# q and k stacks by one transfer, row maxima by one transfer, in a gated attention and MLP kernel

## The chip, the cores and the metric

The kernel runs on one core of a Trainium2 chip. Times are device microseconds (us) of one execution. The engines are named as the profile names them: PE (matmul), PEld (its weight loads), DVE, ACT, POOL, and SP, which here only issues transfers. A transfer is issued by SP or ACT and is carried by the 16 DMA engines of the core.

## The reference

```python
def _A_ref(x, wqkv, wo):                      # x: 1 x 2048 x 512
    H = 32; Dh = 16; W = 256                  # 32 heads of 16 columns, a window of 256 keys
    q, k, v = split(x @ wqkv)                 # each 32 heads x 2048 x 16
    scores = einsum(q, k) * Dh ** -0.5        # masked to 0 <= i - j < 256
    p = softmax(scores)
    return concat(einsum(p, v)) @ wo

def _B_ref(x, w1, b1, w2, b2):                # LayerNorm, 512 -> 1792, GELU, 1792 -> 512
    return gelu(layernorm(x) @ w1 + b1) @ w2 + b2

g = sigmoid((x * gate_w).sum(-1, keepdims=True))
return g * _A_ref(x, ...) + (1 - g) * _B_ref(x, ...)
```

## The kernel before, in words

Every product is made of rounded high parts and remainders (high x high, high x low, low x high), so each operand exists twice. The program has three stages on PE.

**Stage 1, to about 143 us.** `qk_unit(g, t, c)` makes q (t = 0) or k (t = 1) of a group g of 8 heads for a chunk c of 512 tokens, `v_unit(b)` makes v for 128 tokens. Each is 12 matmuls of 512 columns: four with the high part of x and the high part of the weights, four with their low part, and four with the low part of x. `units` is the list of them in order, and `plan` says ahead of which unit a transfer or a fill is issued. For the last chunk of x (c = 3) three of the four low parts are made on POOL (`lo_part` in `load_x`), behind the fills that `masks` and `masks_first` put on POOL's queue; the first unit that reads them is the ninth of the list (`QK(0, 0, 3)`).

`qk_out` sends the high part (twice) and the low part of q or k to `qkd` in HBM. There, one head has 48 rows of 2048 tokens (16 high, 16 high or low, 16 low), and two gap rows of -1 behind them, so 50 rows a head. `gaps(g)` writes these gap rows once for each group, by two transfers, from a part of the stacks tile that `masks` has filled with -1. The calls of `gaps` stand ahead of units 8, 16, 20 and 24, those of `load_stacks` for the first heads ahead of units 11, 19, 29 and 44.

**Stage 2, attention with the first half of the MLP, to about 487 us.** The heads go in eight groups p of four: two pairs `pr`, and in a pair two heads `e`. The tile `qk` (128 partitions, four parts: q of pair 0 and 1, k of pair 0 and 1) holds the stacks: partitions 14 to 61 the 48 rows of the first head of a pair, 64 to 111 those of the second. `load_stacks(p, a, n)` brings n token columns of them, by two transfers of 98 partitions, one for k and one for q. `s_pair` makes the scores of 128 queries and takes their row maxima (DVE); `put_max` splits the maxima in high and low (POOL), turns them (DVE), sends them to HBM, and `rest` brings them back as two rows into the q stacks, by two transfers: one for the high rows (partitions 62 and 112), one for the low rows (63 and 113). `st_pair` makes the transposed scores with these two rows taken along (against the -1 of k), so that the maximum is subtracted in the product; `pv` multiplies by v. The string `ORDER` fixes the order on PE: S is an `s_pair`, T an `st_pair`, P a `pv`, f two matmuls of the MLP (`mlp1_unit`).

**Stage 3.** The second half of the MLP and the output projection.

PE's first scores, the `s_pair` calls for p = 0, stand in stage 1: those for the first block of queries ahead of unit 16, those that need the second and third chunk of stacks later (`ps_x` in the profile). SP issues transfers in the program's order, and eight semaphores are shared by the transfers of SP and ACT, so a transfer is issued after the one eight places ahead of it has landed.

Of the kernel before, what the change touches and what calls it, by code (L numbers as in the profile page):

```python
# [13 lines left out]
F32R = mybir.dt.float32r  # L14
# [5 lines left out]
S = 2048  # L20
D = 512
H = 32
DH = 16
F = 1792
DT = D // 128
KT = D // 64
FT = F // 128
C = 512
NCH = S // C
NB = S // 128  # L30
NG = 4
HG = H // NG
VW = 17
VR = 560
EPS = 1e-5
NEG = -3.0e38
U8 = mybir.dt.uint8
# [24 lines left out]
def gated_mix_kernel(ctx, tc: tile.TileContext, xt, x2, wq0, wqk, wv, wo, xa, gw, w1, w2, b1, b2, out):  # L62
    nc = tc.nc
    dve, act, pool, pe, sp = nc.vector, nc.scalar, nc.gpsimd, nc.tensor, nc.sync
    consts = ctx.enter_context(tc.tile_pool(name="consts", bufs=1))
    dram = ctx.enter_context(tc.tile_pool(name="dram", bufs=1, space=bass.MemoryType.DRAM))
# [3 lines left out]
    def nm(s):  # L70
        uid[0] += 1
        return f"{s}_{uid[0]}"
# [10 lines left out]
    def get(key, tag, bufs, shape, dt=F32):  # L83
        return left[key].tile(list(shape), dt, name=nm(tag), tag=tag, bufs=bufs)
# [3 lines left out]
    def t2(dt=F32, shape=(128, 512)):  # L88
        return get("work", "t", nt[0], shape, dt)
# [36 lines left out]
    def view(t, *ap, off=0):  # L126
        return bass.AP(tensor=t.tensor, offset=t.offset + off, ap=[list(x) for x in ap])

    def f32(t):
        return t.bitcast(F32)  # L130

    def lo_part(lo, src, hi, eng=dve):
        eng.tensor_tensor(out=lo, in0=src, in1=f32(hi), op=ALU.subtract)
# [25 lines left out]
    osc = dram.tile([8, 128, S], F32, name="osc")  # L159
    stat = dram.tile([2, 2, S // 2], F32, name="stat")  # L160
    hp = dram.tile([NCH, FT, 128, C], F32, name="hp")
    qkd = {(g, t): dram.tile([HG, 50, S], F32R, name=f"qk{g}_{t}") for g in range(NG) for t in range(2)}

    open_pool("w")
    open_pool("ring")
    qk = get("ring", "qk", 1, (128, 4, S), F32R)
    qs, ks = [qk[:, pr] for pr in range(2)], [qk[:, 2 + pr] for pr in range(2)]
    vs = get("ring", "v", 1, (128, NB, VR))
    tri = consts.tile([128, 2, 128], U8, name="tri")
# [33 lines left out]
    def masks():  # L203
        for t in qs:
            pool.memset(f32(t[:32]), 0.0)
        for k in ks:
            pool.memset(f32(k[96:128]), -1.0)
        one = small("scr", 2, (128, 256), BF16)
        pool.memset(one, 1.0)
        pool.affine_select(out=one[:, :128], in_=one[:, :128], pattern=[[-1, 128]], base=0, channel_multiplier=1,  # L210
                           compare_op=ALU.is_ge, fill=0.0)
        for e in range(2):
            pool.tensor_copy(tri[:, e], one[:, :128])
        pool.memset(wide, 0.0)
        pool.memset(rt, 0.0)
        pool.affine_select(out=wide[:, 128:], in_=wide[:, 128:], pattern=[[-1, 128]], base=0, channel_multiplier=1,
                           compare_op=ALU.is_ge, fill=NEG)

    def gaps(g):
        for t in range(2):  # L220
            sp.dma_start(f32(view(qkd[g, t], [50 * S, HG], [S, 2], [1, S], off=48 * S)), f32(ks[0][112:128]))

    wq, wvs, xh, xl = {}, [], [], []

# [77 lines left out]
    def qk_unit(g, t, c):  # L302
# [6 lines left out]
                n += 1  # L309
        qk_out(g, t, c, o)  # L310

    def qk_out(g, t, c, o):
        d = qkd[g, t]
        h, l = t2(F32R), t2(F32R)
        copy(h, o)
        lo_part(l, o, h)

        def put(eng, k, s):
            eng.dma_start(f32(view(d, [S, DH], [50 * S, HG], [1, C], off=k * DH * S + c * C)), f32(s))

        if g:
            put(act, 0, h)
        late = (2, 1, 1, 1)[c] if not g else 1
        after(late, lambda: [put(sp, k, h) for k in ((0, 1 + t) if not g else ())])
        after(late, lambda: put(sp, 2 - t, l))

    def double(g, c, t):
        fr, to = (f32(view(qkd[g, t], [S, DH], [50 * S, HG], [1, C], off=k * DH * S + c * C)) for k in (0, 1 + t))
        sp.dma_start(to, fr)

    def v_unit(b):
# [12 lines left out]
    def load_stacks(p, a, n):  # L344
        g, j = divmod(p, 2)
        held_cols[p] = a + n
        for t in (1, 0):
            src = view(qkd[g, t], [S, 98], [100 * S, 2], [1, n], off=4 * j * 50 * S + a)
            sp.dma_start(f32(qk[14:112, 2 * t:2 * t + 2, a:a + n]), f32(src))

    mxs, done = {}, set()

    def s_pair(p, qb, pr):
        if qb == 0 and pr == 0:
            mxs[p] = small("mx", 2, (128, 2, 2, NB))
        assert qb * 128 < held_cols[p]
        n = min(qb + 1, 3) * 128
        t0 = qb * 128 + 128 - n
        o = two()
        for e in range(2):  # L360
            r, k = ((0, 62), (64, 112))[e]
            pe.matmul(o[:, e, :n], qs[pr][r:k, qb * 128:qb * 128 + 128], ks[pr][r:k, t0:t0 + n],  # L362
                      start=True, stop=True)
        m = mxs[p][:, pr, :, qb]
        if qb < 2:
            for e in range(2):
                sc = small("scr", 2, (128, 256), BF16)
                dve.tensor_tensor_reduce(out=sc[:, :n], in0=o[:, e, :n], in1=wide[:, 256 - n:], scale=1.0, scalar=NEG,
                                         op0=ALU.add, op1=ALU.max, accum_out=m[:, e:e + 1])
        else:  # L370
            dve.copy_predicated(o[:, :, :128], tri, o[:, :, 256:384])  # L371
            dve.tensor_reduce(m, o[:, :, :256], mybir.AxisListType.X, ALU.max)  # L372
        if pr and qb % 4 == 3:
            put_max(p, qb - 3)

    def put_max(p, a):
        mx = mxs[p][:, :, :, a:a + 4]
        sm = {}
        md = dram.tile([2, 2, 2, 4, 128], F32R, name=nm("md"))

        def parts():
            m = sm["m"] = small("nm", 2, (128, 2, 2, 2, 4), F32R)
            pool.tensor_copy(m[:, 0], mx)
            lo_part(m[:, 1], mx, m[:, 0], pool)

        def turn():
            sm["s"] = small("ms", 2, (128, 32))
            dve.transpose(sm["s"], f32(sm["m"]).rearrange("p a b c d -> p (a b c d)"))

        def put(eng=None):  # L390
            (eng or (act if spot[0] > 99 else sp)).dma_start(f32(view(md, [32, 4], [128, 32], [1, 32])), sm["s"])

        def rest():
            done.add(("m", p, a // 4))
            for k in range(2):
                src = view(md, [512, 2], [1024, 2], [1, 512], off=2048 * k)
                sp.dma_start(f32(qk[62 + k:113 + k:50, :2, a * 128:a * 128 + 512]), f32(src))

        if spot[0] is None:
            parts()  # L400
            after(1, lambda: (turn(), put(sp)))
            after(3, rest)
        else:
            for n, fn in zip(CHAIN, (parts, turn, put, rest)):
                soon(n, fn)
# [75 lines left out]
    def stat_end(half):  # L481
# [4 lines left out]
        ri = r.bitcast(I32)  # L486
        dve.tensor_scalar(ve, m[:, :, 1], 1.0 / D, EPS, op0=ALU.mult, op1=ALU.add)
        dve.tensor_scalar(ri, ve.bitcast(I32), 1, None, op0=ALU.logical_shift_right)
# [299 lines left out]
    t = spare[0]  # L788
# [115 lines left out]
    for n in range(len(seq)):  # L904
        tick()
        for k in (n + 6,):
            c, f = item(k)
# [4 lines left out]
        c, f = item(n + 1)  # L912
# [6 lines left out]
        c, f = seq[n]  # L919
# [52 lines left out]
```

## Time and profile before

| | us |
|---|---|
| median of 3 runs (lowest, highest) | 689.19 (689.06, 690.45) |
| the profiled execution | 689.64 |
| its span, first to last instruction | 687.8 |
| PE busy | 681.1 |
| DVE, ACT, POOL busy | 476.4, 384.6, 265.9 |

1.8 us of the profiled execution lie outside its span. A span of a matmul in the profile has a modelled end, and matmuls overlap, so PE's busy time is no measure of its rate; its idle time is that in which no matmul was under way. Rows of the views read as: start, length, engine, line, operation, tiles out and in, shape; in brackets the idle time of the engine ahead of it, and who ended it.

### The profile page before, as it was taken

The numbers are of one execution on the slowest core, as the hardware profiler recorded it, in microseconds if no ns is written. First come the engines' busy times: TensorE is split into PE (matmuls) and PEld (weight loads), VectorE is DVE, ScalarE is ACT, GpSimd is POOL, SyncE is SP. The second block draws the span as 40 slices with busy tenths as digits, with TensorE's granted clock in tenths as the row PEclk, the third lists the DMA queues.
The fourth block names the chain that finished last, engine by engine and source line by source line (L and its number), as shares of the span: only waits on it lengthen the run. The fifth ranks groups of instructions, "written<-read, shape, count | busy, mean of one in ns | idle before, by whom it ended". The sixth has DMA issues, their size and how long they took to land.

```text
span 687.8 us, 15593 instructions
## 1 busy us (share of the span) xinstructions
PE 681.1 (99%) x5674; PEld 535.5 (78%) x5674; DVE 476.4 (69%) x970; ACT 384.6 (56%) x637; POOL 265.9 (39%) x622
## 2 busy tenths in 40 slices
PE   9999999999999999999999999999999999999997
PEld 6887777877768777877787777777787888888886
DVE  6737789968777787777686877855575545556454
ACT  6438453457677776877758777687633224123231
POOL 6800156426666664765656566568000000000000
PEclk9999999999999999999999999999999999999999
DMA  8998888786575767566676555527876450841801
GB/s 322 354 290 266 278 262 267 217 253 224 176 211 173 247 211 228 174 214 188 190 240 207 168 185 153 178 96 240 288 238 204 143 173 5 275 126 41 253 1 62
DMA packets 89620, 137.91 MB, mean 200 GB/s; under 512 B 13160, under 2 KB 36648, under 8 KB 89416
## 3 DMA queue, kind: packets, MB, share of 16 engines
q1 hardware_dynamic: 81384, 128.72, 59.1%
q10 hardware_dynamic: 8160, 8.19, 3.9%
q8 instruction: 45, 0.74, 0.4%
q14 instruction: 31, 0.25, 0.1%
HBM read 81.53 MB, written 54.30 MB: 197 GB/s over the span
## 4 chain that ended last, share of the span: by engine, by line
PE 96%; ACT 1%; DVE 1%; DMA 1%; issue 0%; POOL 0%; SPq 0%; DVEq 0%; ACTq 0%
PE ps_b L651 22%; PE ps_a L881 22%; PE ps_b L441 13%; PE ps_d L308 12%; PE ps_b L418 7%; PE ps_b L362 7%; PE ps_d L338 7%; PE ps_o L850 6%; PE ps_d L295 1%; PE ps_x L362 1%; DMA qk<-qk 1%; PE ps_x L279 1%; ACT x L420 0%; DVE us L895 0%; DVE us L889 0%; ACT pb L420 0%
## 5 line engine op out<-in xcount | busy, mean ns | idle before, releaser
L651 PE MATMUL ps_b<-x,w 64*128 64x512 f32 x1344 | 207.1, 393 | 0.0
L881 PE MATMUL ps_a<-x,t 128*128 128x512 f32 x648 | 150.2, 389 | 0.2 <-DVE t L711 0.2
L372 DVE TENSOR_REDUCE mx<-ps_b 128x2 f32<-128x512 f32 x208 | 144.1, 693 | 7.1
L881 PEld LDWEIGHTS ps_a<-x,t 128*128 128x128 f32 x648 | 121.5, 188 | 26.2 <-DVE t L711 0.6
L651 PEld LDWEIGHTS ps_b<-x,w 64*128 64x128 f32 x1344 | 127.4, 186 | 10.5 <-ACT x L136 0.3
L371 DVE COPY_PREDICATED ps_b<-tri,ps_b 128x256 f32<-128x256 uint8 x208 | 88.4, 425 | 52.7 <-PE ps_b L362 40.6
L422 POOL TENSOR_SCALAR_AFFINE_SELECT pa<-pa 128x256 f32<-128x256 f32 x192 | 74.2, 414 | 57.7 <-ACT pa L420 56.7
L420 ACT ACTIVATE pa<-ps_b 128x768 f32<-128x768 f32 x96 | 76.5, 813 | 24.7 <-PE ps_b L418 13.3
L418 PE MATMUL ps_b<-qk 50*128 50x384 f32 (+5 forms) x512 | 87.8, 339 | 0.1
L308 PE MATMUL ps_d<-x,w 128*128 128x512 f32 x360 | 84.7, 390 | 0.0
L362 PE MATMUL ps_b<-qk 62*128 62x384 f32 (+3 forms) x472 | 83.0, 345 | 1.0 <-DMA qk<-qk 0.8
L308 PEld LDWEIGHTS ps_d<-x,w 128*128 128x128 f32 x360 | 67.3, 188 | 14.5 <-issue 0.5
L420 ACT ACTIVATE pb<-ps_b 128x768 f32<-128x768 f32 (+2 forms) x96 | 66.2, 706 | 20.5 <-PE ps_b L418 9.7
L422 POOL TENSOR_SCALAR_AFFINE_SELECT pb<-pb 128x256 f32<-128x256 f32 x160 | 62.2, 415 | 37.4 <-ACT pb L420 36.9
L707 ACT ACTIVATE t<-t,b1s 128x512 f32<-128x512 f32 x56 | 38.6, 716 | 44.0 <-DMA t<-hp 43.6
L418 PEld LDWEIGHTS ps_b<-qk 50*128 50x128 f32 (+1 forms) x512 | 48.8, 184 | 16.0 <-issue 3.2
L422 POOL TENSOR_SCALAR_AFFINE_SELECT x<-x 128x256 f32<-128x256 f32 x128 | 49.3, 414 | 29.7 <-ACT x L420 29.3
L420 ACT ACTIVATE x<-ps_b 128x768 f32<-128x768 f32 x64 | 50.7, 813 | 14.0 <-PE ps_b L418 9.7
L362 PEld LDWEIGHTS ps_b<-qk 62*128 62x128 f32 (+1 forms) x472 | 45.1, 184 | 17.2 <-issue 3.9
L338 PE MATMUL ps_d<-wv,x 128*128 128x512 f32 x192 | 46.7, 394 | 0.0
L850 PE MATMUL ps_o<-w,t 128*128 128x512 f32 x192 | 46.1, 389 | 0.0
L441 PE MATMUL ps_b<-pa,v 128*32 128x128 f32 (+2 forms) x704 | 42.9, 345 | 0.3 <-ACT x L420 0.2
(96 smaller groups left out, 757.1 us busy)
## 6 DMA issues: line engine op xcount, KB each, us to landing
qk<-qk SPq DMA_DIRECT2D x112, 196.0 KB
t<-hp SPq DMA_DIRECT2D x56, 256.0 KB
hp<-t SPq DMA_DIRECT2D x54, 256.0 KB
qk<-t SPq DMA_DIRECT2D x48, 256.0 KB
osc<-x SPq DMA_DIRECT2D x31, 256.0 KB
t<-in_w SPq DMA_DIRECT2D x28, 256.0 KB
w<-w SPq DMA_DIRECT2D x28, 256.0 KB
qk<-t ACTq DMA_DIRECT2D x24, 256.0 KB
```

The lines of the kernel that those rows point to most:

```text
L308: pe.matmul(o, a[:, dt * 128:(dt + 1) * 128], b[:, dt * C:(dt + 1) * C], start=n == 0, stop=n == 11)
L338: pe.matmul(o, x[:, a:a + 128], wvs[dt][:, k], start=n == 0, stop=n == 11)
L362: pe.matmul(o[:, e, :n], qs[pr][r:k, qb * 128:qb * 128 + 128], ks[pr][r:k, t0:t0 + n], start=True, stop=True)
L371: dve.copy_predicated(o[:, :, :128], tri, o[:, :, 256:384])
L372: dve.tensor_reduce(m, o[:, :, :256], mybir.AxisListType.X, ALU.max)
L418: pe.matmul(o[:, e, :w], ks[pr][r:k, kb * 128:kb * 128 + 128], qs[pr][r:k, kb * 128:kb * 128 + w], start=True, stop=True)
L420: act.activation(pt[:, :, :w], o[:, :, :w], AF.Exp, scale=0.25)
L422: pool.affine_select(out=pt[:, :, a:a + 128], in_=pt[:, :, a:a + 128], pattern=[[0, 2], [sgn, 128]], base=b, channel_multiplier=-sgn, comp ...
L441: pe.matmul(a[32 * h:32 * h + 32, at:at + w], vs[:, kb, v:v + 32], pts[p, kb][:, h, fr:fr + w], start=n == 0, stop=n == len(parts) - 1, sk ...
L651: pe.matmul(o[:, e], w[kt // 4][r:r + 64, k, m:m + 128], y[r:r + 64, a:a + C], start=n == 0, stop=n == 23)
L850: pe.matmul(a, x[:, g], wos[g][:, k], start=n == 0, stop=n == 11)
L881: pe.matmul(accs[c][b], x[:, b * 128:(b + 1) * 128], w, start=f == 0 and n == 0, stop=f == FT - 1 and n == 2)
```

## The change

The HBM arrays of q and k of a group become one array, with 52 rows a head (four gap rows). Its heads are ordered anew, by the order of the columns of the weights, so that the four parts q0, q1, k0, k1 of four heads lie at one stride. `load_stacks` brings all four parts by one transfer of 100 partitions: 14 to 61 the first head, 62 to 65 the gap rows, 66 to 113 the second head. The maxima use the gap rows 62 to 65 (high and low of the first head, high and low of the second), so `rest` is one transfer of four partitions. Only the four heads of a group that lie first in a stack have their gap rows written: `gaps` takes rows of 0 for q from partitions 0 to 3 of the stacks tile, and rows of -1 for k from partitions 124 to 127, all four parts of each. So `masks` fills partitions 96 to 127 of all four parts of the tile with -1, by one instruction, where it filled those of the two k parts by two.

```diff
+HR = 52
-    qkd = {(g, t): dram.tile([HG, 50, S], F32R, name=f"qk{g}_{t}") for g in range(NG) for t in range(2)}
+    qkd = [dram.tile([2, HG, HR, S], F32R, name=f"qk{g}") for g in range(NG)]
     def masks():
         for t in qs:
             pool.memset(f32(t[:32]), 0.0)
-        for k in ks:
-            pool.memset(f32(k[96:128]), -1.0)
+        pool.memset(f32(qk[96:128]), -1.0)
     def gaps(g):
         for t in range(2):
-            sp.dma_start(f32(view(qkd[g, t], [50 * S, HG], [S, 2], [1, S], off=48 * S)), f32(ks[0][112:128]))
+            dst = view(qkd[g], [S, 4], [2 * HR * S, 4], [1, S], off=(t * HG * HR + 48) * S)
+            sp.dma_start(f32(dst), f32(qk[124 * t:124 * t + 4]))
+    def rows(g, t, c, k):
+        return view(qkd[g], [S, DH], [HR * S, HG], [1, C], off=(t * HG * HR + k * DH) * S + c * C)
     def qk_out(g, t, c, o):
         def put(eng, k, s):
-            eng.dma_start(f32(view(d, [S, DH], [50 * S, HG], [1, C], off=k * DH * S + c * C)), f32(s))
+            eng.dma_start(f32(rows(g, t, c, k)), f32(s))
     def load_stacks(p, a, n):
         g, j = divmod(p, 2)
         held_cols[p] = a + n
-        for t in (1, 0):
-            src = view(qkd[g, t], [S, 98], [100 * S, 2], [1, n], off=4 * j * 50 * S + a)
-            sp.dma_start(f32(qk[14:112, 2 * t:2 * t + 2, a:a + n]), f32(src))
+        src = view(qkd[g], [S, 100], [4 * HR * S, 4], [1, n], off=2 * j * HR * S + a)
+        sp.dma_start(f32(qk[14:114, :, a:a + n]), f32(src))
     def s_pair(p, qb, pr):
-            r, k = ((0, 62), (64, 112))[e]
+            r, k = ((0, 62), (64, 114))[e]
     def put_max(p, a):
-        md = dram.tile([2, 2, 2, 4, 128], F32R, name=nm("md"))
+        md = dram.tile([4, 2, 4, 128], F32R, name=nm("md"))
         def parts():
             m = sm["m"] = small("nm", 2, (128, 2, 2, 2, 4), F32R)
-            pool.tensor_copy(m[:, 0], mx)
-            lo_part(m[:, 1], mx, m[:, 0], pool)
+            mt = mx.rearrange("p r e b -> p e r b")
+            pool.tensor_copy(m[:, :, 0], mt)
+            lo_part(m[:, :, 1], mt, m[:, :, 0], pool)
         def rest():
-            for k in range(2):
-                src = view(md, [512, 2], [1024, 2], [1, 512], off=2048 * k)
-                sp.dma_start(f32(qk[62 + k:113 + k:50, :2, a * 128:a * 128 + 512]), f32(src))
+            sp.dma_start(f32(qk[62:66, :2, a * 128:a * 128 + 512]), f32(view(md, [1024, 4], [512, 2], [1, 512])))
# in kernel(), the columns of the weights
-    wqk = A_wqkv[:, :2 * D].reshape(DT, 128, 2, NG, HG, DH).transpose(3, 2, 1, 0, 5, 4)
+    wqk = A_wqkv[:, :2 * D].reshape(DT, 128, 2, NG, 2, 2, 2, DH).transpose(3, 2, 1, 0, 7, 5, 4, 6)
```

On POOL the fills of `masks`, and what stands behind them up to the low parts of x (x is the pair of tiles with the high and the low part, v the tile that holds the raw x at that time, qk the stacks), stood in this order before:

```order
L205 MEMSET qk_79 32x2048 x2
L207 MEMSET qk_79 32x2048 x2
L209 MEMSET scr_273 128x256
L210 ISA
L210 AFFINE_SELECT scr_273<-scr_273 128x128
L213 CAST tri<-scr_273 128x128 x2
L214 MEMSET wide 128x256
L215 MEMSET rt 128x32
L216 AFFINE_SELECT wide<-wide 128x128
L583 MEMSET v_80 128x2240
L133 TENSOR_TENSOR x_33_157<-v_80,x_32_156 128x512 x3
```

and now:

```order
L206 MEMSET qk_75 32x2048 x2
L207 MEMSET qk_75 32x8192
L209 MEMSET scr_268 128x256
L210 ISA
L210 AFFINE_SELECT scr_268<-scr_268 128x128
L213 CAST tri<-scr_268 128x128 x2
L214 MEMSET wide 128x256
L215 MEMSET rt 128x32
L216 AFFINE_SELECT wide<-wide 128x128
L584 MEMSET v_76 128x2240
L134 TENSOR_TENSOR x_33_153<-v_76,x_32_152 128x512 x3
```

Nothing changed places; the second fill is one of 8192 columns in place of two of 2048.

On SP, from the second group's gap rows (qk_0_67 and qk_1_68 are its q and k in HBM, qk_79 the stacks tile) to the second chunk of stacks, it was:

```order
L221 DMA qk_0_67<-qk_79 8x2x2048
L221 DMA qk_1_68<-qk_79 8x2x2048
L468 DMA t_588<-in_xa 128x512
L319 DMA qk_1_70<-t_619 16x8x512
L468 DMA t_627<-in_xa 128x512
L468 DMA t_646<-in_xa 128x512
L319 DMA qk_0_71<-t_676 16x8x512
L349 DMA qk_79<-qk_1_66 98x2x512
L349 DMA qk_79<-qk_0_65 98x2x512
```

and it is now:

```order
L222 DMA qk_66<-qk_75 4x4x2048 x2
L469 DMA t_582<-in_xa 128x512
L322 DMA qk_67<-t_613 16x8x512
L469 DMA t_621<-in_xa 128x512
L469 DMA t_640<-in_xa 128x512
L322 DMA qk_68<-t_670 16x8x512
L351 DMA qk_75<-qk_65 100x4x512
```

The gap transfers stay two, with another shape; the two transfers of the stacks became one at the place of the first.

More of the change, by code (lines that the diff above doesn't have):

```diff
@@ L310, in qk_unit @@
         qk_out(g, t, c, o)
+    def rows(g, t, c, k):
+        return view(qkd[g], [S, DH], [HR * S, HG], [1, C], off=(t * HG * HR + k * DH) * S + c * C)
     def qk_out(g, t, c, o):
-        d = qkd[g, t]
         h, l = t2(F32R), t2(F32R)
@@ L327, in double @@
     def double(g, c, t):
-        fr, to = (f32(view(qkd[g, t], [S, DH], [50 * S, HG], [1, C], off=k * DH * S + c * C)) for k in (0, 1 + t))
+        fr, to = (f32(rows(g, t, c, k)) for k in (0, 1 + t))
         sp.dma_start(to, fr)
```

## The prediction

> **What bounds the kernel now.** I read the page's busy times and the chain that ended last first, then who PE waited for.
>
> ```profile
> PE 681.1 (99%) x5674; PEld 535.5 (78%) x5674; DVE 476.4 (69%) x970; ACT 384.6 (56%) x637; POOL 265.9 (39%) x622
> PE 96%; ACT 1%; DVE 1%; DMA 1%; issue 0%; POOL 0%; SPq 0%; DVEq 0%; ACTq 0%
> PE ps_x L279 <- DVE t L275: 1.3, 1, 1.3
> PE ps_b L362 <- DMA qk<-qk: 0.8, 1, 0.8
> PE ps_b L441 <- ACT x L420: 0.2, 1, 0.2
> PE ps_a L881 <- DVE t L711: 0.2, 1, 0.2
> ```
>
> PE is 96% of the chain, and of its waits (the last four rows are the whole list) one is for a transfer that the change touches: 0.8 us for a stack. No row says that PE waits for maxima. So the merging can give PE back 0.8 us at most, however much it saves on SP's queue. A loss has no such bound: what PE reads can come later. I therefore look for what comes later, and the place is stage 1, where the DMA engines are busiest (columns: window, its length, busy time and count of PE, PEld, DVE, ACT, POOL, granted clock, DMA share, GB/s):
>
> ```profile
> 10.00:20.00 10.00, 10.00 (x46) 8.29 (x45) 10.00 (x14) 5.91 (x11) 9.38 (x6) 1.00 1.05 401
> 30.00:34.00 4.00, 4.00 (x20) 3.30 (x19) 1.38 (x2) 1.51 (x3) 3.15 (x2) 1.00 0.84 258
> 34.00:40.00 6.00, 6.00 (x28) 4.99 (x27) 1.81 (x3) 1.52 (x3) 0.00 (x0) 1.00 0.87 232
> 40.00:50.00 10.00, 10.00 (x47) 8.01 (x45) 3.02 (x6) 2.62 (x6) 0.00 (x0) 1.00 0.99 310
> 50.00:60.00 10.00, 10.00 (x48) 7.86 (x48) 7.30 (x25) 8.59 (x22) 0.00 (x0) 1.00 0.93 287
> 60.00:72.00 12.00, 12.00 (x56) 9.08 (x55) 9.40 (x28) 7.37 (x18) 2.55 (x11) 1.00 0.91 287
> 72.00:100.00 28.00, 28.00 (x128) 21.48 (x127) 20.71 (x43) 17.15 (x43) 7.85 (x18) 1.00 0.84 251
> 100.00:108.00 8.00, 8.00 (x37) 6.36 (x37) 7.32 (x14) 2.79 (x6) 6.12 (x9) 1.00 0.87 293
> ```
>
> PE has no idle time from 10 to 108 us, and a DMA share of 0.84 to 0.99 leaves little room to catch up.
>
> **Part 1: the fill of -1 on POOL.** Two fills of 2048 columns become one of 8192.
>
> ```profile
> L583 POOL MEMSET v<- 128x2240 f32 x4 | 7.8, 1978 | 6.2 <-DMA v<-in_xt 6.2
> L207 POOL MEMSET qk<- 32x2048 f32 x2 | 3.6, 1808 | 0.1
> 16.04 3.56 POOL L207 MEMSET qk<- 32x2048 f32 x2
> 21.98 1.98 POOL L583 MEMSET v<- 128x2240 f32 x1
> 25.07 4.25 POOL L133 TENSOR_TENSOR x<-v,x 128x512 fp32r<-128x512 f32 x3 [1.11 <-ACT x L136]
> 28.08 3.11 PE L308 MATMUL ps_d<-x,w 128*128 128x512 f32 x13
> ```
>
> 2048 columns take 1.808 us, 2240 take 1.978: time goes with the columns, so 8192 take about 7.15 us, 3.6 more than the 3.56 of the pair. What stands behind it on POOL runs without idle time to 23.96; the low parts of x waited 1.1 us for ACT, so they move by 3.6 - 1.1 = 2.5 us and end at 29.3 + 2.5 = 31.8. The unit at 28.08 (a matmul each 0.227 us: 2.72 for 12) reads the low parts in its last four, the third of them in its 11th, at 28.08 + 10 x 0.227 = 30.35. PE waits 1.4 us, or 1.0 if the three take 1.3 us each. I take **1.3 us**, near certain as a mechanism. Nothing covers it: PE's queue is in order.
>
> **Part 2: the gap rows.** Eight transfers of 128 KB, two a group, read 4 partitions (32 KB of each) where they read 16. The destination's outer count goes from 8 to 4. The page of the profile has no time to landing for them, so I bound one.
>
> ```profile
> 28.77 1.50 SPq L221 DMA_DIRECT2D qk<-qk  x2
> 55.38 1.39 SPq L221 DMA_DIRECT2D qk<-qk  x2
> 65.32 2.25 SPq L221 DMA_DIRECT2D qk<-qk  x2
> 78.14 1.37 SPq L221 DMA_DIRECT2D qk<-qk  x2
> DMA packets 55, 0.14 MB, mean 283 GB/s; under 512 B 10, under 2 KB 10, under 8 KB 47
> q1 hardware_dynamic: 21, 0.08, 97.4%
> ```
>
> The last two rows are for 80.9 to 81.4 us, behind the fourth group's issue. Eight packets (55 - 47) are of 8 KB, and only these transfers have such; SP's queue, q1, spent 97.4% x 16 x 0.5 = 7.8 us on its packets, so at most 0.97 us on one of 8 KB. At the rate of 10 to 20 us (401 / 16 / 1.05 = 24 GB/s an engine) it would be 0.34. So the packets wait for something that is not the engine, and what eight engines share there is a block of 16 partitions. Estimates: before, 8 engines with two packets each, 0.7 to 1.9 us a transfer. After, four engines with four packets each: 1.4 us if the engine is the limit, and 4 x 1.94 = 7.8 if a partition gives no more than now (a quarter of the partitions, the same bytes). The 0.97 is nearer to a shared source than the 0.34, but it was taken beside other traffic; I take the middle of each, 1.3 before and 4.6 after: 2 x 3.3 = **6.6 us more a group** on the engines that carry them (ends: 2 x 0.7 = 1.4, 2 x 5.9 = 11.8).
>
> [...]
>
> **Part 3: what the stacks in stage 1 then cost PE.** A stack cannot be issued before its gap rows have landed, and stands behind them in the same queue.
>
> ```profile
> 40.74 0.88 SPq L349 DMA_DIRECT2D qk<-qk  x2
> SPq L468 <- DMA qk<-qk: 1.1, 1, 1.1
> 47.17 0.33 SPq L468 DMA_DIRECT2D t<-in_xa  x1
> 49.93 0.44 PE L362 MATMUL ps_x<-qk 62*128 62x128 f32 x4
> 62.69 1.05 SPq L349 DMA_DIRECT2D qk<-qk  x2
> 74.72 0.61 PE L362 MATMUL ps_x<-qk 62*128 62x384 f32 x4
> 94.94 1.06 SPq L349 DMA_DIRECT2D qk<-qk  x2
> 107.79 0.61 PE L362 MATMUL ps_x<-qk 62*128 62x384 f32 x4
> ```
>
> The wait row is for 45 to 48 us: SP waited to 47.17 for the first half of the first stack. The second half, issued 0.4 us behind, landed between 47.6 and 49.9: slack 1.1 (0 to 2.3), some 8 us from issue. By the same 8 us the second stack has 12.0 - 8 = 4 us of slack, the third 12.9 - 8 = 5. A merged stack of about 800 KB saves an issue (0.4 us sooner); if its bytes lie on fewer engines it is later, up to the 1.6 us that lie between two halves of equal size at most. I take 0.6 later. What is idle on the DMA engines takes up lateness: up to 60 us by the share, since 0.99 at 310 GB/s shows that the engines are occupied well under their best rate; behind that by the mean of what share and rate (of 401) leave.
>
> - To 49.9: 6.6 + 0.6 - 1.5 (16% of 30 to 34, 13% of 34 to 40, 1% of ten) = 5.7 late; less 1.1 of slack, PE is **4.6** behind. The 1.3 of part 1 lies inside: PE arrives later at the same wait.
> - To 74.7: 5.7 + 6.6 + 0.6 - 0.7 - 2.3 (19% of 12) = 9.9; less 4 = **5.9** behind.
> - To 107.8, two groups: 9.9 + 13.2 + 0.6 - 7.4 (26.5% of 28) - 1.6 = 14.7; less 5 = **9.7** behind.
>
> Beyond that there are no more gap rows, and the fourth stack (needed at about 150) has time. With the share alone throughout, 14.4; with the rate alone, nothing is left but part 1's 1.3.
>
> **Part 4: stage 2.**
>
> ```profile
> 222.32 2.14 SPq L349 DMA_DIRECT2D qk<-qk  x4
> 222.80 5.36 DMA qk<-qk
> 228.29 0.44 PE L362 MATMUL ps_b<-qk 62*128 62x384 f32 x2 [0.79 <-DMA qk<-qk]
> L349 SPq DMA_DIRECT2D qk<-qk x120: 308/411/2010, 40.7 to 447.5; - x120
> L397 SPq DMA_DIRECT2D qk<-md x64: 596/636/972, 81.3 to 465.8; - x64
> ```
>
> 60 issues of 0.41 and 32 of 0.64 us go: 45 us of SP's queue. They buy PE the 0.79 at best, at 228, where the second half (issued at 222.80, chain row) came last. One transfer is issued at 222.32, 0.5 sooner, but lands as a whole: -0.8 to +0.8, I take **+0.4**. The maxima come back 0.64 sooner; no PE wait hangs on them: 0, and if they came late, `st_pair` would be next to wait. Two more rows in the product, strided POOL copies of 16 columns and the new order of heads: 0, since matmul time goes with columns, and POOL has 61% idle to hide the copies; without that cover, 32 x under 0.1 us.
>
> **Sum.** 9.7 + 0.4 = 10.1 on the profiled execution's 689.64 (span 687.8 and 1.8 around it), which is 0.45 above the median 689.19: against the median, **699.3 us**.
>
> **Rivals.**
>
> - *The gap transfers are no slower than their engines (1.4 us a group more), or hide in idle DMA time.* For it: by the rate, 287 of 401 GB/s, engines are idle 28% at 50 to 72. Against: 0.97 against 0.34 us a packet. PE is left with part 1 and part 4: 1.3 + 0.4, to 4: 691 to 693.
> - *The other side, not slower: POOL's longer fill does no harm and only the wait at 228 goes.* It needs the third low part by 30.35, so the fill would have to cost under 3.6 - 1.4 = 2.2 us more. Then -0.8: 688.4, inside 0.2%. [...] No row of a PE wait leaves more than the 0.8 to gain by it.
> - *The gap transfers at their upper end, 11.8 a group.* Then 5.2 more for each of four groups: about 30 us, 719. For it: the 0.97 row. Against: that row has ACT's traffic beside it.
>
> **How the numbers follow.** A run can tell about 0.2% (1.4 us) from no change. The forecast, 5 to 16 us lost, has 0.60; the first rival 0.18; the upper end, above 16, 0.12; no loss 0.10. Part 1 alone (690.5) is at the bound of what is measured. Range: from 691, part 1 and little else, to 711, which leaves most of the upper end out. Slower 0.87 (all but the last case and a part of the first rival), same 0.10, faster 0.03.
>
> **What would show it.** Part 1: a PE wait of 1.0 to 1.5 us for POOL near 30 us, behind a fill of 7.1 us. Part 2: a low GB/s behind each pair of gap transfers. Part 3: PE waits for `qk<-qk` at the first three stacks, `ps_x` rows at about 54.5, 80.6 and 117.5 in place of 49.9, 74.7 and 107.8, and the attention stage no longer than before. I am wrong if those rows move by the same small amount: then the gap transfers are not slow, or other idle time takes them up.

## The result, and the profile after

| | before | after |
|---|---|---|
| median, us (lowest to highest, runs) | 689.19 (688.97 to 690.45, 5) | 718.14 (715.11 to 720.10, 5) |
| the profiled execution, its span | 689.64, 687.8 | 715.11, 713.1 |

The changed kernel takes 1.0408 times as long, with a 95% interval of 1.0381 to 1.0435: 29 us slower. I had forecast 699.3 us, between 691 and 711. The direction was right, the size was wrong by a factor of nearly three; 719, the figure of the third rival, is where the time came out. The profiled execution is the fastest of the five, so the 25.3 us that are read from its trace below are the smaller end of the loss.

PE's share of the chain and the list of who PE waited for answer to the first rows of the prediction (the last row of the list, of 0.2 us, left out):

```profile
PE 76%; DMA 13%; DVE 6%; ACT 2%; SPq 1%; issue 1%; ACTq 0%; POOL 0%; DVEq 0%
PE ps_x L364 <- DMA qk<-qk: 10.3, 2, 7.1
PE ps_d L309 <- ACT v L137: 3.1, 1, 3.1
PE ps_x L364 <- DVE mx L374: 2.2, 2, 1.6
PE ps_b L364 <- DMA qk<-qk: 1.3, 2, 0.8
PE ps_x L280 <- DVE t L276: 1.3, 1, 1.3
PE ps_d L341 <- DVE wv L236: 0.8, 1, 0.8
PE ps_b L442 <- POOL pb L423: 0.4, 1, 0.4
PE ps_b L364 <- DVE mx L370: 0.3, 1, 0.3
```

PE went from 96% of the chain to 76%, and where one row spoke of the stacks with 0.8 us, two now hold 11.6. The other new rows, for ACT and for DVE, name engines that the change hardly touches. The windows of stage 1 (columns as in the prediction) show where it happens:

```profile
30.00:34.00 4.00, 4.00 (x19) 3.33 (x18) 3.20 (x2) 1.50 (x4) 4.00 (x3) 1.00 0.97 303
34.00:40.00 6.00, 6.00 (x28) 4.96 (x27) 1.98 (x3) 2.31 (x4) 2.47 (x2) 1.00 0.50 116
40.00:50.00 10.00, 10.00 (x46) 8.29 (x45) 1.12 (x2) 1.20 (x2) 0.00 (x0) 1.00 0.69 206
50.00:60.00 10.00, 2.91 (x15) 2.10 (x13) 3.02 (x6) 2.02 (x5) 0.00 (x0) 0.84 0.99 273
60.00:72.00 12.00, 12.00 (x49) 9.45 (x50) 8.51 (x31) 9.90 (x25) 0.00 (x0) 0.85 0.74 230
72.00:100.00 28.00, 24.76 (x104) 18.48 (x103) 14.52 (x36) 12.02 (x30) 3.27 (x15) 0.94 0.69 200
100.00:108.00 8.00, 8.00 (x37) 6.20 (x37) 3.36 (x7) 2.02 (x5) 0.00 (x0) 1.00 0.51 111
108.00:143.00 35.00, 29.68 (x125) 22.56 (x124) 27.68 (x44) 15.33 (x33) 18.94 (x25) 0.95 0.81 249
```

Three things are to be seen. Behind the first pair of gap transfers, 34 to 40, the DMA engines' rate is 116 GB/s where it was 232; at 100 to 108, behind the last pair, it is 111 where it was 293. PE stands still for 7.1 of the ten microseconds from 50 to 60. And the granted clock, 1.00 before, is 0.84 to 0.94 from 50 to 100 and 0.95 from 108 to 143: at 60 to 72 PE is busy throughout and yet does 49 matmuls where it did 56, at 12 / 56 = 0.214 us each 1.5 us lost. By the clock itself PE loses 0.15 x 12 + 0.06 x 28 + 0.05 x 35 = 5.2 us in the three windows from 60 to 72, 72 to 100 and 108 to 143.

The first S of each of the four stacks, and what stood ahead of it in the timeline of PE and of SP's queue:

```profile
23.29 7.73 PE L341 MATMUL ps_d<-wv,x 128*128 128x512 f32 x24 [0.76 <-DVE wv L236]
32.50 1.04 SPq L222 DMA_DIRECT2D qk<-qk  x2
33.60 4.33 SPq L229 DMA_DIRECT2D t<-in_wqk  x1
38.02 5.21 SPq L322 DMA_DIRECT2D qk<-t  x3
48.76 0.31 SPq L351 DMA_DIRECT2D qk<-qk  x1
59.87 0.47 PE L364 MATMUL ps_x<-qk 62*128 62x128 f32 x2 [7.09 <-DMA qk<-qk]
89.44 0.62 PE L364 MATMUL ps_x<-qk 62*128 62x384 f32 x4 [3.22 <-DMA qk<-qk]
113.24 5.99 PE L309 MATMUL ps_d<-x,w 128*128 128x512 f32 x18 [3.14 <-ACT v L137]
131.99 0.62 PE L364 MATMUL ps_x<-qk 62*128 62x384 f32 x4
174.90 0.44 PE L364 MATMUL ps_b<-qk 62*128 62x384 f32 x2 [0.84 <-DMA qk<-qk]
```

The first S come at 59.87, 89.44, 131.99 and 174.90, where they were at 49.93, 74.72, 107.79 and, in the row below, 149.63: 9.9, 14.7, 24.2 and 25.3 us behind. The span is 713.1 - 687.8 = 25.3 longer, so all of the loss is made in stage 1, and the stages behind it took as long as before.

```profile
149.63 0.34 PE L362 MATMUL ps_b<-qk 48*128 48x384 f32 x2
```

In SP's queue the two issues of the gap transfers (L222) are followed by one issue of 4.33 us and three of 5.21; before, what followed took 1.38 and 2.51. What SP issues next stands still too: the stack is issued at 48.76 where it was at 40.74, and from 50 to 60, while PE waits for it, the DMA engines are full again (0.99).

### The profile page after: what moved, and what is told of

It is laid out like the page before. It is cut to its first block, busy times and chain, and to the rows that moved or that the text cites. A ratio compares the mean times of both kernels' runs of the same rounds, so it can differ in the third digit from the quotient of the medians.

```text
span 713.1 us, 15508 instructions
## 1 busy us (share of the span) xinstructions
PE 688.7 (97%) x5674; PEld 537.8 (75%) x5674; DVE 479.6 (67%) x970; ACT 384.3 (54%) x637; POOL 270.5 (38%) x621
## 4 chain that ended last, share of the span: by engine, by line
PE 76%; DMA 13%; DVE 6%; ACT 2%; SPq 1%; issue 1%; ACTq 0%; POOL 0%; DVEq 0%
PE ps_a L882 21%; PE ps_b L652 20%; PE ps_b L442 12%; PE ps_b L419 7%; PE ps_b L364 6%; PE ps_o L851 6%; DMA t<-in_xa 4%; DMA qk<-qk 3%; DMA t<-in_x 2%; PE ps_d L309 2%; PE ps_d L341 2%; DMA t<-in_wqk 2%; DVE x L134 1%; DVE t L533 1%; DVE wv L236 1%
## 5 line engine op out<-in xcount | busy, mean ns | idle before, releaser
L882 PEld LDWEIGHTS ps_a<-x,t 128*128 128x128 f32 x648 | 121.6, 188 | 25.3
L423 POOL TENSOR_SCALAR_AFFINE_SELECT pa<-pa 128x256 f32<-128x256 f32 x192 | 74.2, 414 | 56.3 <-ACT pa L421 55.3
L309 PE MATMUL ps_d<-x,w 128*128 128x512 f32 x360 | 89.6, 406 | 3.1 <-ACT v L137 3.1
L309 PEld LDWEIGHTS ps_d<-x,w 128*128 128x128 f32 x360 | 70.5, 197 | 19.5 <-ACT v L137 3.6
L421 ACT ACTIVATE x<-ps_b 128x768 f32<-128x768 f32 x64 | 50.7, 813 | 15.0 <-PE ps_b L419 10.9
L341 PE MATMUL ps_d<-wv,x 128*128 128x512 f32 x192 | 48.5, 399 | 1.1 <-DVE wv L236 0.8
L341 PEld LDWEIGHTS ps_d<-wv,x 128*128 128x128 f32 x192 | 35.4, 188 | 11.9 <-DVE wv L236 2.0
```

Of the source, the lines that this page charges most:

```text
L309: pe.matmul(o, a[:, dt * 128:(dt + 1) * 128], b[:, dt * C:(dt + 1) * C], start=n == 0, stop=n == 11)
L341: pe.matmul(o, x[:, a:a + 128], wvs[dt][:, k], start=n == 0, stop=n == 11)
L421: act.activation(pt[:, :, :w], o[:, :, :w], AF.Exp, scale=0.25)
L423: pool.affine_select(out=pt[:, :, a:a + 128], in_=pt[:, :, a:a + 128], pattern=[[0, 2], [sgn, 128]], base=b, channel_multiplier=-sgn, comp ...
L882: pe.matmul(accs[c][b], x[:, b * 128:(b + 1) * 128], w, start=f == 0 and n == 0, stop=f == FT - 1 and n == 2)
```

## The experiments

The theory after this trace was: the gap transfers, read from four neighbouring partitions, are slow at their source; while a pair of them runs, nearly all other transfers stand still, and the idle time that they leave cannot be used. The rivals were that the count of engines (four for the gap rows, ten for the merged stacks) is what is slow, that SP's queue is, or that the merged transfers have a price of their own. A second theory was for the fill on POOL. All are compared with the kernel before, run on the same chip.

Two readings below go beyond the views: the trace also keeps when the semaphore of a transfer goes up. Apart from a step as the issue ends, where there is one, the semaphore of a gap transfer goes up in eight steps in the kernel before, in four in after, and in sixteen where the transfer reads 64 partitions; that of a stack goes up in fourteen steps for each half before and in ten in after. For the gap transfers before and after these are the counts of engines that the prediction reckons with, so I take the steps as the engines that carry a transfer, which is an estimate of mine, and the last step as its landing (the first stack's in after comes at 59.82, PE's first S at 59.87). From the first issue to the landing of both, the first pair of gap transfers takes 5.5 us before (28.77 to 34.26) and 12.0 in after (32.50 to 44.50).

| kernel | median, us | ratio to before (95%) |
|---|---|---|
| before + gap rows from four neighbouring partitions | 721.34 | 1.0463 (1.0421 to 1.0505) |
| before + gap rows, destination written as four pieces | 690.14 | 1.0007 (0.9988 to 1.0026) |
| before + one long fill | 693.23 | 1.0039 (1.0021 to 1.0057) |
| after, gap rows from 64 partitions | 694.32 | 1.0073 (1.0053 to 1.0094) |
| after, gap rows from every fourth partition | 698.71 | 1.0117 (1.0072 to 1.0162) |
| after, gap rows in pieces of 2 KB, from four neighbouring partitions | 720.07 | 1.0426 (1.0373 to 1.0478) |
| after, gap rows issued by ACT | 720.27 | 1.0429 (1.0381 to 1.0478) |
| after, the fill in four | 720.54 | 1.0438 (1.0399 to 1.0477) |
| after, further matmuls in PE's waits | 717.83 | 1.0393 (1.0345 to 1.0441) |
| after, gap rows from 64 partitions, no long fill | 691.20 | 1.0013 (0.9996 to 1.0030) |
| the same, stacks of q and k apart | 690.38 | 0.9999 (0.9985 to 1.0013) |
| the same as the last but one, maxima by two | 693.91 | 1.0049 (1.0025 to 1.0072) |

**Is it the gap rows alone?** Into the kernel before, only the gap transfers were put that the change has, which read four neighbouring partitions on four engines:

```diff
-            sp.dma_start(f32(view(qkd[g, t], [50 * S, HG], [S, 2], [1, S], off=48 * S)), f32(ks[0][112:128]))
+            dst = view(qkd[g, t], [100 * S, 4], [50 * S, 2], [S, 2], [1, S], off=48 * S)
+            src = view(qk, [list(qk.ap)[0][0], 4], [0, 2], [1, 2 * S], off=124 * list(qk.ap)[0][0] + 2 * S)
+            sp.dma_start(f32(dst), f32(src))
```

> The kernel before, with one thing changed: the two gap transfers of each group read four partitions (each one's 4 x 2048 values of -1 twice over the same two stacks) and start on four engines, as in the changed kernel; stacks, maxima and the fill stay as before. Theory (the slow gap transfers carry nearly all of the loss: 25.3 us less 2.8 us of the fill): 706 to 714 us, the gap transfers land some 10 us after issue (5.3 before), and the first S of stage 1 comes 6 to 10 us later than at 49.93. Rival (the gap transfers cost the 7 us that I forecast, and the rest is the merged loads with their ten engines): 695 to 699 us.

Measured: 721.34 us, with stacks, maxima and the fill as before. The gap rows by themselves cost as much as the whole change. That is above the 714 of my theory, and the delay at the first stack is a little smaller than I said (its S comes at 55.3, 5.4 us later); the list of PE's waits shows why:

```profile
PE ps_d L310 <- ACT v L136: 8.4, 1, 8.4
PE ps_x L364 <- DVE mx L374: 7.7, 6, 4.8
PE ps_x L364 <- DMA qk<-qk: 5.5, 1, 5.5
```

Only 5.5 us are waits for a stack; 16.1 are for ACT and DVE. In the trace of after the same chain can be followed. ACT's copies stand behind its statistics (L472, L473), which wait for a transfer, and DVE's dots and maxima stand behind ACT's:

```profile
111.13 0.63 ACT L472 ACTIVATE waste<-t 128x512 f32<-128x512 f32 x1 [9.07 <-DMA qk<-t]
112.60 0.58 ACT L137 ACTIVATE v<-ps_d 128x512 f32<-128x512 f32 x1
112.73 0.69 DVE L476 SCALAR_TENSOR_TENSOR t<-t,gws 128x512 f32<-128x512 f32 x1 [7.21 <-ACT waste L473]
```

ACT waited 9.07 us for its input, and PE's wait of 3.14 at 113.24 is for the copy at 112.60 behind it. So whatever comes by a transfer in this stage is late, and not the stacks alone.

**Engines or partitions?** The destination written as four pieces, as in the last kernel, the source left at 16 partitions:

```diff
-            sp.dma_start(f32(view(qkd[g, t], [50 * S, HG], [S, 2], [1, S], off=48 * S)), f32(ks[0][112:128]))
+            dst = view(qkd[g, t], [100 * S, 4], [50 * S, 2], [S, 2], [1, S], off=48 * S)
+            sp.dma_start(f32(dst), f32(ks[0][112:128]))
```

> The kernel before, with the destination of the gap transfers cut into four pieces instead of eight, so that four engines move them, while the source stays 16 partitions of 8 KB. Theory (the four source partitions make it slow, not the count of engines): 689 to 692 us, four engines move 128 KB in about 1.2 to 2.5 us each. Rival (four engines are what is slow): as b_gap4, over 700 us.

Measured: 690.14, no difference from before. But it is no test of four engines, for the edit changed nothing: four pieces of two heads each name the same rows in the same order as eight of one head, and the semaphores still go up in eight steps. The opposite was meant to be sixteen engines from four partitions, in the changed kernel:

```diff
-            dst = view(qkd[g], [S, 4], [2 * HR * S, 4], [1, S], off=(t * HG * HR + 48) * S)
+            dst = view(qkd[g], [512, 16], [2 * HR * S, 4], [1, 512], off=(t * HG * HR + 48) * S)
```

> The changed kernel with the destination of its gap transfers cut into sixteen pieces, so that sixteen engines move them, while the source stays four neighbouring partitions. Theory (the four partitions' rate limits): a transfer still takes some 4.6 us, now on all sixteen engines, and the time is 710 to 730 us. Rival (four engines with 8 KB pieces in a row are the limit): 692 to 697 us.

Measured: 720.07, as slow as the change. Here too the count of engines stayed, at four steps; what changed is the size of a packet, 2 KB in place of 8. So smaller pieces do not help; whether more engines would, no run here shows. And four partitions again, with 32 KB of each on four engines, but every fourth one:

```diff
-            sp.dma_start(f32(dst), f32(qk[124 * t:124 * t + 4]))
+            row = list(qk.ap)[0][0]
+            sp.dma_start(f32(dst), f32(view(qk, [4 * row, 4], [1, 4 * S], off=112 * t * row)))
```

> The changed kernel with its gap transfers reading again four partitions of 32 KB on four engines, but every fourth partition (0, 4, 8, 12 for q; 112, 116, 120, 124 for k) in place of four neighbours. Theory (four neighbouring partitions share one way out of the buffer; the source's place is what is slow): 692 to 695 us, which is what the fill alone leaves, and the gap transfers land within 4 to 8 us. Rival (few partitions with 32 KB each are slow wherever they lie): 713 us or more.

Measured: 698.71. Engines (four steps), bytes and packets (8 KB) are those of after, and only the place of the partitions differs: it takes off 718.14 - 698.71 = 19.4 us, two thirds of the loss. So four engines by themselves are not what makes the change slow. The first pair of gap transfers takes 6.9 us (33.14 to 40.01), 1.4 more than before. The time is 3.7 us above what I expected at most, so this cure is not whole: 8.5 us over before are left, of which the fill, tested below, is 3.2. Four engines may be part of the rest, which no run shows. The DMA engines' rate from 34 to 44 us, in forty slices of 0.25 us, for before, after, packets of 2 KB from four partitions, and every fourth partition:

```profile
GB/s 254 287 361 352 295 303 262 295 344 221 188 131 148 156 143 74 135 107 157 135 225 290 340 362 369 413 402 401 402 401 402 418 393 410 336 295 270 221 188 197
```

```profile
DMA  9993563330330603209859440230203206998759
GB/s 344 336 311 131 172 115 33 33 33 0 33 33 0 66 0 33 33 0 139 180 188 320 164 90 8 66 57 0 66 0 66 33 0 139 205 205 287 213 180 287
```

```profile
GB/s 344 336 328 385 328 172 25 33 25 25 25 25 33 25 25 16 33 25 25 33 98 106 147 295 221 82 41 33 33 33 33 33 33 33 33 25 82 221 188 270
```

```profile
GB/s 402 377 393 377 369 230 205 229 115 41 221 311 254 295 221 221 213 295 229 254 262 303 328 352 320 369 279 229 147 74 90 66 115 112 202 225 273 312 300 372
```

33 GB/s in a slice is one packet of 8 KB (8192 bytes in 0.25 us). In after, the twelve slices from 35.5 to 38.5 sum to 297, a mean of 24.8 GB/s for all sixteen engines together, while the `DMA` row gives them as idle for most of it; with packets of 2 KB, fourteen slices from 35.5 to 39 give 26.6. So the gap transfers run at one low rate with packets of either size. The window from 35.5 to 38.5 of after alone:

```profile
DMA packets 11, 0.07 MB, mean 25 GB/s; under 512 B 2, under 2 KB 2, under 8 KB 2
```

Nine packets of 8 KB begin in it and two under 512 B, so for three microseconds no other transfer moves data beside the gap rows. Before, the lowest slice is 74. That the place of the four partitions decides is shown by 698.71 us against 718.14; a way out that neighbours share, as the theory for that run has it, is in no row.

**Is it SP's queue?** The changed kernel's gap transfers issued by ACT:

```diff
-            sp.dma_start(f32(dst), f32(qk[124 * t:124 * t + 4]))
+            act.dma_start(f32(dst), f32(qk[124 * t:124 * t + 4]))
```

> The changed kernel with the gap transfers issued by ACT, whose queue carries nothing else in this stage, in place of SP. Theory (what stands behind a gap transfer waits for two reasons: SP's queue holds eight in flight and four engines are kept busy; the first falls away): 702 to 712 us. Rival A (the queue is all: the transfers behind run on freely): 692 to 697 us. Rival B (the four engines are all): within 2 us of 718.1.

Measured: 720.27, 0.2 us beyond the bound of rival B and far from the others. ACT's queue is not as empty as I had written: from 52 us on it carries a part of q's and k's transfers, but at the first pair nothing else. SP's own issues are held although the gap transfers are not in its queue:

```profile
34.06 0.88 ACTq L222 DMA_DIRECT2D qk<-qk  x2
35.66 8.18 SPq L322 DMA_DIRECT2D qk<-t  x3
```

Three issues of SP's took 8.18 us behind ACT's two. By which way the slow transfers hold up those of another queue is not shown by any run here; that they do is. Nor does this run tell rival B's four engines from the four neighbouring partitions; the run with every fourth partition does.

**The gap rows cured, the fill kept.** A source of 64 partitions, in columns of the stacks tile that are loaded last:

```diff
         pool.memset(f32(qk[96:128]), -1.0)
+        for t in range(2):
+            pool.memset(f32(qk[64:128, 2 * t, 1536:]), -t)
...
-            dst = view(qkd[g], [S, 4], [2 * HR * S, 4], [1, S], off=(t * HG * HR + 48) * S)
-            sp.dma_start(f32(dst), f32(qk[124 * t:124 * t + 4]))
+            dst = view(qkd[g], [512, 16], [2 * HR * S, 4], [1, 512], off=(t * HG * HR + 48) * S)
+            sp.dma_start(f32(dst), f32(qk[64:128, 2 * t, 1536:]))
```

> The changed kernel with gap transfers from 64 partitions (512 values each, in columns of the stacks that are loaded last) on sixteen engines; the fill of 32 x 8192 is kept, and two small fills of 64 x 512 come behind it. Theory: the loss shrinks to what the fill costs, 2.8 us: 691 to 693.5 us, and the wait at the first S of stage 1 under 1 us. Rival (merged loads and ten engines carry part of it): 697 us or more.

Measured: 694.32. It is 24 us under the change and 5 over before (689.35 there), 0.8 above my interval and below the rival's. I put what is left down to the fill, which is longer here, since the two small fills, 1.4 us together, stand behind it; the run without the long fill, further down, bears this out.

**The fill.** In the kernel before, the one long fill alone:

```diff
-        for k in ks:
-            pool.memset(f32(k[96:128]), -1.0)
+        pool.memset(f32(qk[96:128]), -1.0)
```

> The kernel before with its two fills of 32 x 2048 written as the one fill of 32 x 8192. Theory (DVE's casts of wv wait until POOL's fills have ended, whether these are one or four, and PE's units of V come later by that): the first cast 6.3 us in place of 2.96, 691 to 693 us. Rival (the lag is taken up in stage 1, where the matmuls wait on nothing else): 689 to 690 us.

Measured: 693.23, 3.2 above the 690.01 of before in that set and 0.2 above my interval. PE's unit of V, before and with the long fill:

```profile
22.64 5.60 PE L338 MATMUL ps_d<-wv,x 128*128 128x512 f32 x24
23.45 7.75 PE L337 MATMUL ps_d<-wv,x 128*128 128x512 f32 x24 [0.46 <-DVE wv L234]
```

It ends at 31.20 in place of 28.24. And the changed kernel with its fill in four instructions:

```diff
-        pool.memset(f32(qk[96:128]), -1.0)
+        for i in range(4):
+            pool.memset(f32(qk[96:128, i]), -1.0)
```

> The changed kernel with its fill of 32 x 8192 written as four fills of 32 x 2048: the same time on POOL, but four instructions. Theory (DVE's casts of wv can't run beside one long fill, and slip in between short ones): the casts at 17 us come back from 7.7 to about 4 us mean, PE's unit at 28 us is 1.5 to 2.8 us earlier, 715.3 us or little more. Rival (POOL's total time counts, through what stands behind the fill on POOL): within 1 us of 718.1.

Measured: 720.54, no gain, and above the rival's bound too; the theory that DVE slips in between the four was wrong. The timelines of DVE's casts of `wv` and POOL's fills: one row of before, three of after (its cast behind the operation ahead of it), three of the four fills (the last one starts at 16.96 like the one above it, and holds two casts):

```profile
16.93 2.96 DVE L235 CAST wv<-t 128x512 fp32r<-128x512 f32 x1
```

```profile
16.00 6.95 POOL L207 MEMSET qk<- 32x8192 f32 x1
16.29 0.68 DVE L134 TENSOR_TENSOR t<-ps_d,t 128x512 fp32r<-128x512 f32 x1
16.89 6.34 DVE L236 CAST wv<-t 128x512 fp32r<-128x512 f32 x1
```

```profile
16.07 7.33 POOL L208 MEMSET qk<- 32x2048 f32 x4
16.96 2.94 DVE L237 CAST wv<-t 128x512 fp32r<-128x512 f32 x1
16.96 6.71 DVE L237 CAST wv<-t 128x512 fp32r<-128x512 f32 x2
```

The first cast of after takes 6.34 us and ends 0.28 behind the fill's end (16.89 + 6.34 against 16.00 + 6.95). Before, the pair of fills ended at 19.60 and the cast at 19.89. With four fills a cast ends at 19.90, behind the second, and the next at 23.67, behind the fourth: here one gets in at every second end only. Without a long fill the four casts take 1.80 us together, in the run further down. The `TENSOR_TENSOR` at 16.29 took 0.68 us beside the running fill, so the fill does not hold every operation of DVE; what about the cast decides is not shown by a run.

**The half clock.** Further matmuls fill PE's two waits for stacks:

```diff
         o = two()
+        for _ in range({(0, 0): 26, (0, 4): 10}.get((p, qb), 0) if pr == 0 else 0):
+            pe.matmul(o[:, 1], xh[0][:, :128], xh[0][:, :512], start=True, stop=True)
```

> The changed kernel with 26 further matmuls (128 x 512, their result is overwritten) ahead of the first S of stage 1, and 10 ahead of that of its fifth block, where PE stands idle for 7.1 and 3.2 us; the output is as before. Theory (the granted clock of 0.5 over 3.4 to 6.8 us, in which matmuls take 427 ns in place of 227, comes from the idle stretches before): the two stretches of half clock behind these waits are gone, and with them about 3 us, though the third stays: 713 to 717 us. Rival (the half clock has another cause): the stretches are as before and the time is within 1 us of 718.1 or above it by the further matmuls.

Measured: 717.83, 0.8 above my interval and inside the rival's; in the time nothing can be told. Its trace, the wait at the first S and three windows:

```profile
62.70 0.69 PE L366 MATMUL ps_x<-qk 62*128 62x128 f32 x4 [3.93 <-DMA qk<-qk]
50.00:60.00 10.00, 8.76 (x39) 6.93 (x37) 3.02 (x6) 2.02 (x5) 0.00 (x0) 1.00 0.97 264
60.00:72.00 12.00, 9.30 (x34) 7.19 (x35) 6.22 (x20) 7.34 (x19) 0.00 (x0) 0.72 0.78 250
72.00:100.00 28.00, 26.90 (x119) 20.16 (x118) 15.02 (x43) 13.92 (x36) 3.29 (x15) 1.00 0.66 185
```

In this run the stack came later (62.70 against 59.87), so that 3.93 us of waiting were left behind the 26 matmuls, and a stretch at a low clock followed it (0.72 at 60 to 72). At the fifth block, where ten matmuls stand ahead of S, the clock stays at 1.00 (72 to 100) where after had 0.94. That speaks for the idle time as the cause at one of two places, and gives no saving.

**Do the merged transfers cost or bring anything?** The changed kernel with the wide source and without the long fill:

```diff
-        pool.memset(f32(qk[96:128]), -1.0)
+        for t in range(2):
+            pool.memset(f32(qk[64:128, 2 * t, 1536:]), -t)
```

> The changed kernel with gap transfers from 64 partitions (512 values each, in columns of the stacks that are loaded last) on sixteen engines, and without the fill of 32 x 8192: two fills of 64 x 512 are in its place (0.74 us each in the run that kept the large fill). Theory (slow gap transfers and the fill are the whole loss): 688 to 691 us, no wait of PE for the low parts of wv, and the first S of stage 1 within 1 us of 49.93. Rival (the merged stacks and maxima cost something of their own, as the 694.3 of the run that kept the large fill may say, 5 us over before where the fill explains 2.8): 692 us or more.

Measured: 691.20, 0.2 above my interval and below the rival's; 1.0013 times before (0.9996 to 1.0030). The first S comes at 49.73. The whole list of PE's waits, and DVE's casts:

```profile
PE ps_x L281 <- DVE t L277: 1.3, 1, 1.3
PE ps_b L443 <- POOL pb L424: 0.4, 1, 0.4
PE ps_b L443 <- ACT x L422: 0.2, 1, 0.2
16.91 1.80 DVE L237 CAST wv<-t 128x512 fp32r<-128x512 f32 x4
```

No wait for a transfer is left, the 0.8 us of before included, and the span is 687.4 against 687.8. From this kernel, each merge was undone alone:

```diff
-        src = view(qkd[g], [S, 100], [4 * HR * S, 4], [1, n], off=2 * j * HR * S + a)
-        sp.dma_start(f32(qk[14:114, :, a:a + n]), f32(src))
+        for t in (1, 0):
+            src = view(qkd[g], [S, 100], [4 * HR * S, 2], [1, n], off=(t * HG + 2 * j) * HR * S + a)
+            sp.dma_start(f32(qk[14:114, 2 * t:2 * t + 2, a:a + n]), f32(src))
```

> As the run without the large fill and with wide gap transfers, but the stacks of q and of k come by a transfer each, on ten engines each. Theory (the merge of the stacks is worth between -0.8 and +0.8 us, as forecast for stage 2): within 1 us of that run. Rival (the merged transfer lands later than the second of two, and holds up S at its batches): this one 1 to 3 us faster.

```diff
-            sp.dma_start(f32(qk[62:66, :2, a * 128:a * 128 + 512]), f32(view(md, [1024, 4], [512, 2], [1, 512])))
+            for k in range(2):
+                src = view(md, [1024, 2], [512, 2], [1, 512], off=2048 * k)
+                sp.dma_start(f32(qk[62 + 2 * k:64 + 2 * k, :2, a * 128:a * 128 + 512]), f32(src))
```

> As the run without the large fill and with wide gap transfers, but the maxima of a batch return by two transfers again. Theory (the merged return is worth nothing that can be measured, since maxima land long before they are read): within 1 us of that run. Rival (one issue less on SP's queue matters): 1 to 3 us slower.

Measured: 690.38 with the stacks apart, within what can be told, and 693.91 with the maxima by two. The latter's runs lie between 689.15 and 701.97; without the highest, which the ratio leaves out, their median is 693.15, 2 us over that with one transfer. Its profiled execution has a span of 687.4, the same as with one transfer, so whether this is a price of the second transfer stays open. No version here beats the kernel before by more than can be measured.

## Why the prediction went wrong, point by point

- **What can be gained: right.** I said 0.8 us at most, as only one wait of PE hung on these transfers. With the two faults cured the merges bring the 0.8 us wait down to none and the time to 1.0013 of before.
- **Part 1, the fill: the size of the fill right (6.95 for 7.15), the way wrong, the price too small.** I looked only at what stands behind it on POOL, the low parts of x, and found 1.3 us. No such wait came, though I had called the mechanism near certain. The fill holds DVE's casts (6.34 us for the first in after, 2.96 before), PE's unit of V waits for `wv` (7.73 us from 23.29 where it took 5.60 from 22.64), and alone this costs 3.2 us. I also said that it lies inside the wait at the first stack. It does not: with the long fill alone the gap transfers are issued at 32.7 in place of 28.8, so all behind them moves too.
- **Part 2, the gap rows: right that they are slow, and right in size, but partly by luck.** I took 4.6 us for a transfer of 128 KB. At 24.8 to 26.6 GB/s it is 131072 / 25.7 = 5.1, and the first pair took 12.0 - 5.5 = 6.5 us more, where I had 6.6. But my 4.6 was the middle of two ends, and the reason of the upper one, that a partition gives no more than before, is not what is slow: four partitions with the same bytes each, set apart, needed 1.4 us more for the first pair, which is my lower end. That the four are neighbours decides (718.14 us against 698.71 with every fourth one), and my sum had no term for their place. The eight and four engines in it are the steps of the semaphores in the traces of before and after.
- **Part 3 is the step that failed: "What is idle on the DMA engines takes up lateness".** I subtracted 1.5, 3.0 and 9.0 us for idle time of the engines, with what was left over handed from group to group, and so had the first three stacks come 5.7, 9.9 and 14.7 us late. They landed 10.4, 17.8 and 25.7 us late (at 59.82, 89.30 and 127.92, where it was 49.39, 71.53 and 102.19). Without the subtraction my own terms give 7.2, 14.4 and 28.2; with the 3.7 us by which the fill has the first gap transfers issued later they are 10.9, 18.1 and 31.9. So up to the second stack idle time took up next to nothing, and up to the third about 6 us of the 13.5 that I had subtracted in all. The rows show why: the idle time arises because transfers stand still behind the slow pair (24.8 GB/s on engines that are mostly idle), so it was not there to catch up in. PE was 9.9, 14.7 and 24.2 us behind. At the first two it waited for the stack; the third stack had landed 4 us ahead of its S, and there PE was behind by the waits of the next point as well. The 0.6 us that I took for a merged stack on fewer engines is shown by no run: its semaphore goes up in ten steps in place of fourteen, but with the gap rows and the fill cured the time is 691.20 us with merged stacks and 690.38 with the stacks apart, within what can be told.
- **What I had not counted.** Inputs of ACT's statistics are late as well, which PE feels as waits for ACT and DVE (3.1 and 2.2 us in after, 8.4 and 7.7 with the gap rows alone). Beside PE's waits of 7.1, 3.2 and 3.1 us there are stretches at a granted clock of 0.50, 5.2 us of its work by the windows above. In PE's time the 25.3 us add up about so: 10.8 more of waits for stacks, 6.8 of waits for ACT, DVE and POOL, 5.2 by the clock and 2.1 in the longer unit of V. What each alone would save is not shown: the run with further matmuls in the waits got nothing back.
- **Part 4, stage 2: right.** I took +0.4 us; the shift is 25.3 us at 174.90 and 25.3 at the end. No wait of PE for maxima came.
- **The rivals.** The third one named the right time for the wrong reason: its 11.8 us a group rested on slower transfers than there are (6.5 more for the first pair). The range left it out by giving the absorption by idle time most of the weight, with no row that had shown idle time to be usable behind a slow transfer.

## What to carry to other kernels

Look at a transfer's source partitions as closely as at its bytes: here, one that read four neighbouring partitions ran at 24.8 GB/s, and while it did, other transfers stood still, those of another queue included. Idle time of DMA engines in a profile is not always capacity; behind the slow transfers of this kernel it was a symptom. Look into the trace whether an edit did what it was meant to: two of the runs here were meant to change the count of engines and left it as it was. And a fill on POOL is to be weighed against what DVE does beside it, in that very stretch (here a cast of 6.34 us beside a fill of 6.95), not only against POOL's own queue.

## What the runs showed of the hardware that I had not expected

- With two transfers of 128 KB from four neighbouring partitions under way, all sixteen engines together moved 24.8 GB/s for three microseconds on end in after (718.14 us); packets of 2 KB (26.6 GB/s, 720.07 us) or another issuing queue (720.27 us) did not help, every fourth partition in as many steps did (698.71 us).
- A cast on DVE waited for a running fill on POOL, a `TENSOR_TENSOR` did not (6.34 us against 0.68 in after), and beside four fills in a row the casts got in at every second end only (19.90 and 23.67).
- The granted clock of after stood at 0.50 in three stretches of stage 1, each in or soon behind a wait of PE: from 56.7 to 63.6 us, 4.0 us into the wait of 7.1 that ended at 59.87; from 90.9 to 94.3, 1.4 behind the wait of 3.2 that ended at 89.44; from 114.8 to 118.2, 1.5 behind that of 3.1 that ended at 113.24. In the first, matmuls of 512 columns began 427 ns apart where it is 227 at a clock of 1.00. The waits up to 1.4 us in the run with every fourth partition left the clock at 1.00.
